# Attention with channels on the partitions, fp32 products and dues from formulas, ahead of a routed MoE and an MLP

## The chip, the cores and the metric

One core of one Trainium2 chip. The metric is the time of one execution on the device in microseconds (us): the median of three runs of the kernel before is 1163.12 us (1162.36 to 1168.79). PE is TensorE (PEld its weight loads), DVE is VectorE, ACT ScalarE, POOL GpSimd, SP SyncE, which issues the DMAs.

## What is computed

Three layers follow one another. The first is a recurrent attention over 768 tokens, for 4 x 8 heads of dimension 40:

```
for t in range(768):
    y[t] = r[t] . state
    Sa = state . a[t]
    state = state * w[t] - Sa (x) b[t] + v[t] (x) k[t]
```

Its output, 3072 rows of 320, goes through a mixture of experts (a skip gate, the argmax of 8 experts, 320 to 1024 to 320 with relu, weighted by the gate and added to the row) and then through an MLP, 320 to 2048 to 320, with g = h / (1 + exp(-1.702 h)).

## The kernel before

**Attention** (class `Attn`, L102) takes 12 chunks of 64 tokens, all 32 heads at a time, and turns the recurrence into matrix products. Within a chunk the decays are normalised at its middle (`g_prep`, scans L244 and L256), a, k and b are scaled by them (`g_a`, `g_kb`), and the products of a with k and b make a triangular system. Tokens lie on the partitions. Operands of TensorE are split into fp16 parts, hi, hi and lo side by side on 120 rows; POOL makes the lo parts (L314, L344, L411, L451, L503, L535, L980), and a, k, b, r, v and the state are turned by transposing DMAs from the SP queue (L319, L351, L541, L708, L719, L984).

**The solve** (`g_gram`, L385 to L402) inverts the 32 x 32 diagonal blocks of all heads of one chunk on DVE. L385 brings the system into Z; Tm starts from a POOL memset (L380) and two ACT copies (L383); then 31 steps follow, each a product tmp <- Tm, Z (L396) and a sum Tm <- Tm, tmp (L399), each waiting for the one ahead of it, all of it in SBUF; L402 turns the inverse back. Its parts go into `te` by DMA.

**The chain** (`g_chain`) makes u of the chunk by products with `te` and `bo` (L593 and others) with ACT copies as parts between them, and then the state after the chunk. `g_pq` and `g_post` make y: the masked products of r with v and u (L738, L741) times km (L763, the one fp32 product of attention), plus the state's share (L766), scaled into xo (L772). `put` (L976 to L998) stores xo as parts for the experts' gather and computes the logits.

**Experts and MLP.** `Moe1` routes the rows, loads and splits the weights, and runs 8 experts (L1263 and others); `Moe2` runs blocks of 512 rows (L1512 to L1515 in, L1552 to L1554 out).

**Order.** Every stage is a generator that yields what its next step takes of an engine (`'P.63*.96'`: 0.63 us of TensorE) or an event or a PSUM slot that it waits for. `weave` (L818) steps them in the order in which they can start by these costs, and among steps that could start nearly together takes the one that is due first. So each engine gets one fixed queue, in order. The dues come from the table `RANK` (L1574), one number for each generator; the formulas in `Attn.DUE` and in the module's `DUE` are there, but not used. `g_warm` issues filler products (L792) where the modelled TensorE pauses. PSUM slots are three of a kind c, three of a kind g (five later), and two of X (gx0, gx1).

## Time and profile before

| what | us |
|---|---|
| median of three runs | 1163.12 |
| span of the profiled execution | 1164.9 |
| PE busy in the span | 929.5 |
| DVE busy | 797.7 |
| ACT busy | 497.2 |
| POOL busy | 473.1 |

The profile shows one execution, whose span is 1164.9 us and whose granted clock is 0.833 on average. Busy times are sums over the span; the stages of this kernel have different limits, so a share of the whole span says little. The columns are read by stage.

### The profile page before, as it was taken

To read this page: it belongs to the slowest core of one execution; us is meant where nothing else is said; L and a number is where in the kernel's file an instruction comes from. 1 tells how busy PE (TensorE), PEld (TensorE's weight loads), DVE (VectorE), ACT (ScalarE), POOL (GpSimd) and SP (SyncE) were. 2 spreads that over 40 slices of the span, in tenths; PEclk is the share of its full clock that TensorE was granted. 3 is DMA by queue.
4 is the path that set the end of the run, shared out by engine and by line. 5 is a ranking of instruction groups with operands and counts; after the bars stand their busy time and mean duration, and the time that the engine had idled before them with its cause. 6 is when DMAs were issued, how large, how long until landed. Compare 5 with 4: busy or idle time off the path is not lost.

```text
span 1164.9 us, 27321 instructions
## 1 busy us (share of the span) xinstructions
PE 929.5 (80%) x11343; PEld 654.4 (56%) x11343; DVE 797.7 (68%) x1655; ACT 497.2 (43%) x987; POOL 473.1 (41%) x405
## 2 busy tenths in 40 slices
PE   5757788598787877968840298995979999999998
PEld 5647667486566675756640176672335555555556
DVE  6599999999999999988658986766972111121110
ACT  2324555445544545436424456442543332333330
POOL 4343345435455544445313635442443332333330
PEclk8776777776777786689855599997989999999999
DMA  6564589799889798865796687434300101010000
GB/s 174 138 152 81 102 169 180 166 160 169 194 154 175 147 186 136 187 111 107 132 258 176 225 192 214 152 130 113 94 26 12 28 22 37 12 29 13 12 12 31
DMA packets 301625, 140.08 MB, mean 120 GB/s; under 512 B 271652, under 2 KB 284712, under 8 KB 299432
## 3 DMA queue, kind: packets, MB, share of 16 engines
q1 hardware_dynamic: 299192, 133.91, 52.8%
q0 software_dynamic: 2304, 4.36, 1.3%
...
## 4 chain that ended last, share of the span: by engine, by line
DVE 37%; PE 37%; DMA 11%; issue 7%; POOL 3%; ACT 3%; SPq 2%; POOLq 0%; DVEq 0%; ACTq 0%
DVE tmp L396 8%; DVE Tm L399 8%; PE c L1552 5%; PE c L1553 4%; PE c L1554 4%; PE g L1512 4%; PE g L1515 3%; PE gx L1512 3%; DMA w2s<-w 3%; PE gx L1515 2%; PE g L763 2%; PE gx L792 2%; DVE pq L741 2%; DMA d_s<-wia 1%; DMA g_x<-xd,g_ig 1%
## 5 line engine op out<-in xcount | busy, mean ns | idle before, releaser
L1535 POOL TENSOR_TENSOR glo<-g,ghi 128x512 f16<-128x512 f32 x96 | 113.8, 1187 | 221.9 <-ACT ghi L1534 221.8
L396 DVE SCALAR_TENSOR_TENSOR tmp<-Tm,Z 128x78 f32<-128x78 f32 (+21 forms) x372 | 148.9, 410 | 8.6 <-ACT Tm L383 3.0
L399 DVE TENSOR_TENSOR Tm<-Tm,tmp 128x78 f32<-128x78 f32 (+21 forms) x372 | 146.7, 405 | 5.1
L792 PE MATMUL gx<-c 128*128 128x192 f16 x840 | 131.6, 300 | 6.4 <-DMA c<-c 3.5
L1531 DVE SCALAR_TENSOR_TENSOR g<-g,sg 128x512 f32<-128x512 f32 x57 | 39.2, 688 | 133.3 <-ACT sg L1529 133.3
L1552 PE MATMUL c<-wo_hi,ghi 128*128 128x320 f16 x384 | 115.9, 302 | 5.9 <-ACT wo_hi L1457 5.9
L1553 PE MATMUL c<-wo_lo,ghi 128*128 128x320 f16 x384 | 115.1, 300 | 0.9 <-DVE wo_lo L1460 0.9
L1554 PE MATMUL c<-wo_hi,glo 128*128 128x320 f16 x384 | 115.2, 300 | 0.0
L792 PEld LDWEIGHTS <-c 128*128 128x128 f16 x840 | 82.0, 116 | 39.5 <-issue 30.1
L1534 ACT CAST ghi<-g 128x512 f16<-128x512 f32 x96 | 59.2, 618 | 76.1 <-DVE g L1531 76.1
L1531 DVE SCALAR_TENSOR_TENSOR g<-gx,sg 128x512 f32<-128x512 f32 x39 | 26.9, 689 | 89.9 <-ACT sg L1529 89.9
L451 POOL TENSOR_TENSOR gkl<-m,gkh 64x512 f16<-64x512 f32 x48 | 58.5, 1218 | 58.7 <-ACT gkh L449 46.4
L1512 PEld LDWEIGHTS <-wi_hi 128*128 128x128 f16 x480 | 45.6, 99 | 60.2 <-DMA xt<-xe 13.3
L763 PE MATMUL g<-km,pq 128*64 128x40 f32 x768 | 58.1, 261 | 26.2 <-DVE pq L741 26.1
L1512 PE MATMUL g<-xt,wi_hi 128*128 128x512 f16 x285 | 71.5, 382 | 1.3 <-DVE g L1531 1.3
L763 PEld LDWEIGHTS g<-km,pq 128*64 128x64 f32 x768 | 54.9, 172 | 29.4 <-DVE pq L741 28.4
L1515 PEld LDWEIGHTS <-wi_lo 128*128 128x128 f16 (+1 forms) x288 | 27.8, 97 | 64.1 <-issue 41.6
L1529 ACT ACTIVATE sg<-g 128x512 f32<-128x512 f32 x57 | 33.7, 595 | 64.2 <-PE g L1515 64.2
L1198 POOL TENSOR_TENSOR w2l<-w2s,w2h 128x1280 f16<-128x1280 f32 x16 | 42.9, 2687 | 44.2 <-ACT w2h L1196 44.0
L1512 PE MATMUL gx<-xt,wi_hi 128*128 128x512 f16 x195 | 49.6, 386 | 12.9 <-DMA xt<-xe 12.9
L1552 PEld LDWEIGHTS <-ghi 128*128 128x128 f16 x384 | 37.5, 98 | 28.6 <-issue 16.1
L1515 PE MATMUL g<-xt,wi_lo 128*128 128x512 f16 x171 | 52.1, 382 | 0.0
...
## 6 DMA issues: line engine op xcount, KB each, us to landing
...
```

The source lines that it names most:

```text
L396: nc.vector.scalar_tensor_tensor(out=tv, in0=Tm[:, r0:, st:st + 1].to_broadcast([128, n, st]), scalar=-2.0 ** -18, in1=Z3[:, st:st + 1, 0: ...
L399: nc.vector.tensor_tensor(out=Tm[:, r0:, 0:st], in0=Tm[:, r0:, 0:st], in1=tv, op=ALU.add)
L763: mm(d, lhsT=self.pq[:, q], rhs=km[:, 40 * p:40 * p + 40], start=h == 0, stop=False, **kw)
L792: self.nc.tensor.matmul(self.X[:, 320:], lhsT=self.C['c_i'][:, 0], rhs=self.C['c_rep'].rearrange('p a b -> p (a b)')[:, :192], start=first ...
L1512: nc.tensor.matmul(h, lhsT=self.whi[:, k % 3, fs], rhs=xt[:, k], start=k == 0, stop=False)
L1515: nc.tensor.matmul(h, lhsT=self.wlo[:p, k, fs], rhs=xt[:p, k], start=False, stop=k == 2)
L1531: nc.vector.scalar_tensor_tensor(out=g, in0=h, scalar=2.0 ** -6, in1=sg2, op0=ALU.mult, op1=ALU.mult)
L1534: nc.scalar.copy(out=ghi[:, f], in_=g)
L1535: nc.gpsimd.tensor_tensor(out=glo[:, f], in0=g, in1=ghi[:, f], op=ALU.subtract)
L1552: nc.tensor.matmul(o, lhsT=ghi[:, f, s], rhs=self.ohi[:, f], start=f == 0, stop=False)
L1553: nc.tensor.matmul(o, lhsT=ghi[:, f, s], rhs=self.olo[:, f], start=False, stop=False)
L1554: nc.tensor.matmul(o, lhsT=glo[:, f, s], rhs=self.ohi[:, f], start=False, stop=f == 15)
```

## The change

Attention is written anew; the code of the experts and the MLP stays, apart from the order in which it is queued.

- Channels, not tokens, lie on the partitions for a, k, b, w and r: the host lays them out so. Products are fp32, so no hi and lo parts are made, and there are no transposing DMAs in attention. What must be turned (the decays F, km, v and u, the state, xo for the logits) goes through TensorE with an identity (L247, L286, L556, L534, L834) and an ACT copy.
- POOL scales a and kb (L261, L275, 1024 elements a partition each) and still makes the lo part of xo in `put`.
- `g_gram` takes a pair of chunks. Z of both (L322) lies side by side, Tm lies in a PSUM bank pair of its own, filled by two matmuls from a constant (L328), and each of the 31 steps is one product (L336) and one subtraction (L339) for both chunks. One Z and one Tm are there, so a pair's Z waits for the solve of the pair ahead, and its Tm for the Tc (L345) of the pair ahead.
- The chain is 5 blocks of 16 products of 64 x 64 with 40 columns for each half of the heads: two into X (L441, L448), then `times` (L462) with tz, bz and tz, one ACT copy between each. `tz` has one buffer, filled from Tc by DMA (L354). Consecutive products of a block go to the two column halves of TensorE by turns (`both`: h outside, par inside).
- The state of both halves is one product with the identity and 16 products per parity (L506, L510), scaled by DVE (L514). y is L575, L577, L598, L603 and L609.
- PSUM slots are four of kind g, six later; c0 and c1 are opened after attention.
- `RANK` goes; `weave(A, z)` takes the dues of the formulas, with `T` = 33 and new numbers in `Attn.DUE`.

Counts in the program: PE instructions with their loads 20888 before, 7866 after; DVE 1666 and 1104; solve operations 744 and 372; fillers 840 and 552.

```diff
-    SLOTS = dict(c=3, g=3, s=1, m=1, v=1, x=1)
...
+    SLOTS = dict(g=4, c=0)
...
+        W = self.tile([128, 2, 1024], F32, 'W', 2)
+        wf, wb = W[:, 0], W[:, 1]
+        nc.vector.tensor_tensor_scan(out=wf, data0=wt[:, 0], data1=C1, initial=0.0, op0=ALU.mult, op1=ALU.add)
...
+        nc.vector.tensor_tensor_scan(out=wb[:, rv], data0=wt[:, 1, rv], data1=C2[:, rv], initial=0.0, op0=ALU.mult, op1=ALU.add)
...
+        self.nc.gpsimd.tensor_tensor(out=t, in0=t, in1=self.ch[c]['W'][:, 0], op=ALU.mult)
...
+        for q in range(2):
+            yield 'G2.4'
+            t = kbT[:, 4 * q:4 * q + 4].rearrange('p a b (e t) -> p (a b) e t', e=2)
+            w = W[:, 4 * q:4 * q + 4].rearrange('p a b t -> p (a b) t').unsqueeze(2).to_broadcast([128, 8, 2, 64])
+            nc.gpsimd.tensor_tensor(out=t, in0=t, in1=w, op=ALU.mult)
...
+                for h in range(4):
+                    nc.tensor.transpose(out=ps[:, 128 * h:128 * h + 128], in_=kbT[:, 4 * q + h, par], identity=self.C['c_id'])
...
+    def g_gram(self, c0):
+        nc, mm = self.nc, self.nc.tensor.matmul
+        pair = range(c0, c0 + 2)
+        for i, c in enumerate(pair):
...
+                yield 'P.9*1.9'
+                Ad = self.pst(sg)
+                for h in range(8):
                     for par in range(2):
+                        for half in range(2):
+                            q = 64 - 64 * par + 32 * half
+                            mm(Ad[q:q + 32, 32 * h:32 * h + 32], lhsT=kbT[r, h, par, q:q + 32],
+                               rhs=at[r, h, par, 32 * half:32 * half + 32], start=True, stop=True)
+                yield 'A.26'
+                nc.scalar.copy(out=Za[:, hb], in_=Ad[:, :256])
                 self.give(sg)
...
+            if not i:
+                yield ('elim', c0 - 2)
+                Z = self.tile([128, 2, 1024], F32, 'Z')
+            yield 'D1.2'
+            nc.vector.transpose(out=Z[:, i], in_=Za.rearrange('p b (g t) -> p t (b g)', t=32).unsqueeze(2).to_broadcast([128, 32, 2, 16]))
+        Z4 = Z.rearrange('p q (s j) -> p q s j', j=32)
+        yield ('tT', c0 - 2)
+        yield 'P.43*1.0'
+        Tm = self.pt.tile([128, 2, 16, 32], F32, name='tm')
         for i in range(2):
+            mm(Tm[:, i].rearrange('p a b -> p (a b)'), lhsT=self.C['c_i'], rhs=self.C['c_tm'], start=True, stop=True)
+        tmp = self.tile([128, 272], F32, 'tmp')
         for st in range(31, 0, -1):
             r0 = st // 2
             n = 16 - r0
+            tv = tmp[:, :2 * n * st].rearrange('p (q a b) -> p q a b', q=2, b=st)
+            d = f'D{.06 + 2 * n * st / 960}'
             yield d
+            nc.vector.tensor_tensor(out=tv, in0=Tm[:, :, r0:, st:st + 1].to_broadcast([128, 2, n, st]),
+                                    in1=Z4[:, :, st:st + 1, 0:st].to_broadcast([128, 2, n, st]), op=ALU.mult)
             yield d
+            nc.vector.tensor_tensor(out=Tm[:, :, r0:, 0:st], in0=Tm[:, :, r0:, 0:st], in1=tv, op=ALU.subtract)
+        self.mark('elim', c0)
+        yield ('te', c0 - 3)
+        Tc = self.tile([128, 2, 512], F32, 'Tc', 2)
+        for i in range(2):
+            yield 'D1.0'
+            nc.vector.transpose(out=Tc[:, i].rearrange('p (g t d) -> p t d g', t=16, d=2), in_=Tm[:, i].rearrange('p a b -> p (a b)'))
+        self.mark('tT', c0)
         yield ('zero', 0)
+        tz = self.tz.rearrange('p (a u) t -> p a u t', a=2)
+        for i, c in enumerate(pair):
+            yield ('U', c - 1)
+            yield 'Q2.4>E1.2'
+            for q in range(4):
+                sl = slice(32 * q, 32 * q + 32)
+                nc.sync.dma_start(out=tz[sl, 1 - q // 2, :, q % 2 * 32:q % 2 * 32 + 32], in_=Tc[sl, i].rearrange('p (u t) -> p u t', t=32))
+            self.mark('te', c)
...
+        for h in range(8):
+            for par in range(2):
+                R = slice(64 * par, 64 * par + 64)
+                nc.tensor.matmul(ps[R, 64 * h:64 * h + 64], lhsT=kbT[r, h, par, R], rhs=at[r, h, par], start=True, stop=True)
         yield 'D.6'
+        m = self.tile([128, 8, 64], F32, f'm{hb}', 2)
...
+        yield 'P.95*1.3'
         X = self.X = self.pst(f'gx{hb}')
+        for h, par, p, d, o in both:
+            mm(X[o, d], lhsT=m[:, h], rhs=vu[:, p], start=h == 0, stop=False, **kw)
+        self.mark(f'Xm{hb}', c)
+        yield ('S', c - 1)
         ST = self.state[c]
+        r = slice(64 * hb, 64 * hb + 64)
+        yield 'P.95*1.3'
+        for h, par, p, d, o in both:
+            mm(X[o, d], lhsT=at[r, h, par], rhs=ST[r, 8 * par + h], start=False, stop=True, **kw)
...
+            w = w.rearrange('p (a u) t -> p a u t', a=2)
+            for h, par, p, d, o in both:
+                mm(z[o, d], lhsT=w[:, par, hb * 8 + h], rhs=t[:, h], start=start and h == 0, stop=True, **kw)
+        yield 'A.33'
+        x = part('x', X, -1.0)
+        yield '+g'
         sc = self.got
+        yield 'P.95*1.3'
         U = self.pst(sc)
+        times(U, self.tz, x, True)
+        yield 'A.33'
+        u = part('y', U, 1.0)
+        yield 'P.95*1.3'
+        times(X, self.bz[c % 2], u, True)
         self.mark(f'B{hb}', c)
+        yield 'A.33'
+        x = part('x', X, -1.0)
         self.mark(f'D{hb}', c)
+        yield 'P.95*1.3'
+        times(U, self.tz, x)
         self.once('U', c)
...
+            mm(ps, lhsT=self.C['c_id'], rhs=ST[:, 8 * par:8 * par + 8].rearrange('p a b -> p (a b)'), start=True, stop=False, **kw)
+            for h in range(8):
+                for hb in range(2):
+                    p = hb * 16 + par * 8 + h
+                    mm(ps[64 * hb:64 * hb + 40, 40 * h:40 * h + 40], lhsT=km[:, p], rhs=vu[:, p], start=False, stop=True, **kw)
...
+        yield 'P.9*1.0'
         ps = self.pst(sg)
+        for j in range(4):
+            i = hb * 8 + par * 4 + j
+            nc.tensor.matmul(ps[:, 128 * j:128 * j + 128].rearrange('p (e t) -> p e t', e=2), lhsT=vt[:, i], rhs=rT[:, :, i], start=True, stop=True)
...
+        yield 'P.95*1.3'
         Y = self.pst(sg)
+        for h in range(8):
+            for par in range(2):
                 d = Y[64 * par:64 * par + 64, 40 * h:40 * h + 40]
+                e = 64 * (h % 2)
+                mm(d, lhsT=self.pq[0][:, 4 * par + h // 2, e:e + 64], rhs=km[:, hb, par, h], start=h == 0, stop=False, **kw)
+        S = self.S
+        yield 'P.95*1.3'
+        for h in range(8):
+            for par in range(2):
+                mm(Y[64 * par:64 * par + 64, 40 * h:40 * h + 40], lhsT=rT[:, h % 2, hb * 8 + par * 4 + h // 2],
+                   rhs=S[:, par * 4 + h // 2, 64 * hb:64 * hb + 40], start=False, stop=True, **kw)
...
+    T = 33.0
+    DUE = dict(zero=-63, load=-75, prep=-66, f=-40, a=-62, kb=-60, gram=-56, ag=-20, ab=-8, v=-20, r=-12, chain=-24, state=-10, sn=4, vt=4, pq=8, post=14, put=22)
...
-RANK = [
-    -404.17427774566124, -491.09060918509874, 1000000000.0, -501.3257727435962, 975.1942770611722, 988.2493608546714, 644.544040243994,
...
-    881.3447098714629, 682.3957237723041, 316.5416932928976, 1095.6692978068609, 1665.069538024102, -225.02167154120986, 383.8421061879434,
-    1343.707675234579, 926.7659247826618, 880.8505466156354, 1708.9576193963935, 887.0972506490499, 582.1332617647189, 2281.6272860544195,
...
                 A.left.close()
                 N.open_out(octx)
+                more = actx.enter_context(tc.tile_pool(name='b_ps', bufs=1, space=PS))
+                A.ps = Banks(A.ps, c0=more, c1=more)
                 M.open_x(xctx, tc, A.ps)
-                for t in ('gx0', 'gx1'):
+                for t in ('gx0', 'gx1', 'c0', 'c1'):
...
-            weave(A, [(d, g) for d, (n, g) in zip(RANK, z)])
+            weave(A, z)
```

Where the solve stands on DVE, before (L385 and L396/L399 of one chunk between those of another; the number at the end of a name is the tile's):

```order
L385 STREAM_TRANSPOSE Z_4148<-g0_4059 128x1024
L772 SCALAR_TENSOR_TENSOR xo_4183<-g2_3946,F_661 128x320
L396 SCALAR_TENSOR_TENSOR tmp_4154<-Tm_4149,Z_4148 128x31
L399 TENSOR_TENSOR Tm_3430<-Tm_3430,tmp_3435 128x14x5
L399 TENSOR_TENSOR Tm_4149<-Tm_4149,tmp_4154 128x31
L396 SCALAR_TENSOR_TENSOR tmp_3435<-Tm_3430,Z_3429 128x56
L396 SCALAR_TENSOR_TENSOR tmp_4154<-Tm_4149,Z_4148 128x30
L399 TENSOR_TENSOR Tm_3430<-Tm_3430,tmp_3435 128x14x4
L399 TENSOR_TENSOR Tm_4149<-Tm_4149,tmp_4154 128x30
L396 SCALAR_TENSOR_TENSOR tmp_3435<-Tm_3430,Z_3429 128x45
L396 SCALAR_TENSOR_TENSOR tmp_4154<-Tm_4149,Z_4148 128x58
```

and after (L322 is Z, L514 the state, L577 and L374 masked products):

```order
L230 TENSOR_TENSOR scl_115<-tots_114 128x8x2
L322 STREAM_TRANSPOSE Z_2724<-Za_3017 128x1024
L514 TENSOR_TENSOR ST_3067<-g0_3171,scl_115 128x320
L336 TENSOR_TENSOR tmp_3200<-tm_3197,Z_2724 128x62
L339 TENSOR_TENSOR tm_3197<-tm_3197,tmp_3200 128x2x31
L336 TENSOR_TENSOR tmp_3200<-tm_3197,Z_2724 128x60
L339 TENSOR_TENSOR tm_3197<-tm_3197,tmp_3200 128x2x30
L336 TENSOR_TENSOR tmp_3200<-tm_3197,Z_2724 128x116
L339 TENSOR_TENSOR tm_3197<-tm_3197,tmp_3200 128x2x2x29
L336 TENSOR_TENSOR tmp_3200<-tm_3197,Z_2724 128x112
L577 TENSOR_TENSOR pq_113<-g1_3225,c_32_86 128x512
L339 TENSOR_TENSOR tm_3197<-tm_3197,tmp_3200 128x2x2x28
```

Before, two chunks' solves of single operations alternate; after, one solve of a pair runs with doubled operations, and other work stands between its steps.

On PE, the end of chunk 3 before the solve of chunks 4 and 5 (L312 the system's products, L506 and L510 the state, L328 the fill of Tm, L448 the state's products into X of chunk 4):

```order
L312 MATMUL g2_3134<-at2_98,kbT1_100 32x32 x32
L506 MATMUL g0_3171<-ST_2568,c_32_86 128x320
L510 MATMUL g0_3171<-vu_2182,km_2059 40x40 x16
L556 MATMUL g1_3191<-c_32_86,vu_2182 80x128 x4
L328 LDWEIGHTS c_16_88
L328 MATMUL tm_3197<-c_16_88 128x512
L328 LDWEIGHTS c_16_88
L328 MATMUL tm_3197<-c_16_88 128x512
L448 MATMUL gx0_3035<-ST_3067,at1_97 64x40 x16
L575 MATMUL g1_3225<-rT1_102,vt_2952 128x128 x4
L286 MATMUL g2_3233<-c_32_86,kbT1_100 128x128 x4
```

The fill of Tm stands behind the state after chunk 3, and the X products of chunk 4 stand right behind it. Before, there is no such fill, and y's products stand so behind those of the chain (L593; L763 with all eight of a parity together, 16 in all, then L766):

```order
L593 LDWEIGHTS te_101
L593 MATMUL c2_4802<-xh0_4757,te_101 128x40
L763 MATMUL g1_4822<-km_1043,pq_108 64x40 x16
L766 LDWEIGHTS rT_4615
L766 MATMUL g1_4822<-S0_3855,rT_4615 64x40
```

The sixteen fp32 products of y go to one column half eight at a time before; after, they alternate.

## Rows read from the trace of the kernel before

**Rows 1.** Stretches: length, then busy us of PE, PEld, DVE, ACT, POOL, PEclk, DMA.
```profile
96.00:562.00 466.00, 371.65 (x7266) 307.28 (x7265) 439.73 (x1046) 234.43 (x548) 221.94 (x200) 0.76 0.81 154
664.00:806.00 142.00, 122.05 (x894) 88.17 (x892) 109.07 (x182) 68.76 (x93) 63.07 (x40) 0.94 0.58 169
```

**Rows 2.** Attention's last DVE step per chunk, and the stores of its rows: counts, first and last start.
```profile
L402 DVE STREAM_TRANSPOSE tmp<-Tm x12: 1034/1049/1091, 96.2 to 562.2; 128x512 f32<-128x512 f32 x12
L772 DVE SCALAR_TENSOR_TENSOR xo<-g,F x24: 427/480/493, 149.7 to 617.3; 128x320 f32<-128x320 f32 x24
L385 DVE STREAM_TRANSPOSE Z<-g x12: 1227/1242/1250, 44.5 to 518.5; 128x1024 f32<-128x1024 f32 x12
```

**Rows 3.** VectorE by line, 96 to 562 us: busy us, mean ns of one.
```profile
L399 DVE TENSOR_TENSOR Tm<-Tm,tmp 128x96 f32<-128x96 f32 (+20 forms) x334 | 133.3, 409 | 4.5
L396 DVE SCALAR_TENSOR_TENSOR tmp<-Tm,Z 128x91 f32<-128x91 f32 (+20 forms) x332 | 131.6, 405 | 8.2 <-ACT Tm L383 3.0 <-DVE Tm L399 0.3 <-DVE tmp L396 0.2
...
L256 DVE TENSOR_TENSOR_SCAN wt<-wt,c_d 128x640 f32<-128x640 f32 x8 | 12.8, 1599 | 0.0
```

**Rows 4.** VectorE from 303.15 us in order of time: start, us, operation.
```profile
303.15 1.18 DVE L396 SCALAR_TENSOR_TENSOR tmp<-Tm,Z 128x81 f32<-128x81 f32 x1
304.37 1.48 DVE L399 TENSOR_TENSOR Tm<-Tm,tmp 128x81 f32<-128x81 f32 x1
...
308.59 0.26 DVE L396 SCALAR_TENSOR_TENSOR tmp<-Tm,Z 128x100 f32<-128x100 f32 x1
308.89 0.26 DVE L399 TENSOR_TENSOR Tm<-Tm,tmp 128x100 f32<-128x100 f32 x1
```

**Rows 5.** GpSimd in the same stretch.
```profile
302.95 1.29 POOL L411 TENSOR_TENSOR Tm<-tmp,Tm 128x512 f16<-128x512 f32 x1 [2.97 <-ACT Tm L409]
304.20 1.54 POOL L340 TENSOR_TENSOR km<-km,FK 128x640 f32<-128x640 f32 x1
```

**Rows 6.** VectorE, two lines with a PSUM source, then one without: ns min/median/max.
```profile
L741 DVE TENSOR_TENSOR pq<-g,c x48: 647/680/692, 143.1 to 606.9; 128x512 f32<-128x512 f32 x48
L1048 DVE TENSOR_TENSOR r_e<-g,c_et x5: 156/191/216, 323.8 to 636.3; 128x64 f32<-128x64 f32 x2, 128x16 f32<-128x16 f32 x2, 128x32 f32<-128x32 f32 x1
L1051 DVE TENSOR_TENSOR r_e<-r_e,r_oh x5: 161/209/2575, 324.1 to 636.7; 128x64 f32<-128x64 f32 x2, 128x16 f32<-128x16 f32 x2, 128x32 f32<-128x32 f32 x1
```

**Rows 7.** TensorE in 280.5 to 282.8 us: fp32 products of y (L763), then L766 between them.
```profile
280.70 1.68 PE L763 MATMUL g<-km,pq 128*64 128x40 f32 x29
...
282.20 0.23 PE L763 MATMUL g<-km,pq 128*64 128x40 f32 x1
282.20 0.22 PE L766 MATMUL g<-S,rT 120*64 120x40 f16 x2
282.26 0.23 PE L763 MATMUL g<-km,pq 128*64 128x40 f32 x1
```

**Rows 8.** The same products at 288.44 us, and the granted clock of both stretches.
```profile
288.44 2.92 PE L763 MATMUL g<-km,pq 128*64 128x40 f32 x29
280.70:282.30 1.60, 1.60 (x39) 1.60 (x37) 1.60 (x4) 1.57 (x4) 0.00 (x0) 1.00 1.14 216
288.40:291.20 2.80, 2.80 (x34) 2.76 (x35) 2.73 (x5) 0.94 (x2) 1.70 (x1) 0.50 1.11 126
```

**Rows 9.** Transposes by TensorE, what starts next, and fillers, in order of time.
```profile
297.30 0.55 PE L269 MATMUL g<-c,wt 128*128 128x128 f32 x3
297.69 0.27 PE L992 MATMUL g<-wgh,xt 128*128 128x9 f16 x5
298.05 1.00 PE L792 MATMUL gx<-c 128*128 128x192 f16 x10
```

**Rows 10.** GpSimd and ScalarE by line, 96 to 562 us.
```profile
L340 POOL TENSOR_TENSOR km<-km,FK 128x640 f32<-128x640 f32 x18 | 28.1, 1563 | 0.2 <-DMA km<-raw 0.2
...
L380 POOL MEMSET Tm<- 128x512 f32 x10 | 5.3, 525 | 1.9 <-DMA te<-Tm 1.6
...
L585 ACT ACTIVATE xl<-gx 128x320 f16<-128x320 f32 x44 | 18.8, 433 | 19.8 <-PE gx L589 17.8 <-PE gx L792 1.5
```

More of the change, by code (lines that the diff above doesn't have):

```diff
@@ L214, in load @@
-    def load(self, n, c):
-        a, w = self.args, dict(wt=1280, am=640, km=1280)[n]
-        src = dict(wt=lambda: a['wt'][c].rearrange('q p a b -> p q (a b)'), am=lambda: a['raw'][c, :, :640],
-                   km=lambda: a['raw'][c, :, 640:])[n]()
-        t = self.tile([128, w], F32, n, self.KM if n == 'km' else 1)
-        t = t.rearrange('p (q x) -> p q x', q=2) if n == 'wt' else t
-        for q in range(2) if n == 'wt' and not c else (slice(None), ):
-            self.nc.sync.dma_start(out=t[:, q], in_=src[:, q])
-        self.ch.setdefault(c, {})[n] = t
@@ new lines, in g_v @@
+        yield ('Sx', c - 2)
+        yield 'Q.6>E3.2'
+        vu = self.tile([128, 32, 40], F32, 'vu', 2)
+        self.nc.sync.dma_start(out=vu.rearrange('p a x -> p (a x)'), in_=self.args['rv'][c])
+        self.ch[c]['vu'] = vu
+        self.mark('v', c)
+    def g_r(self, c):
+        yield ('Y', c - 2)
+        for e in range(2):
+            yield 'Q.6>E.8'
+            self.nc.sync.dma_start(out=self.rT[c % 2][40 * e:40 * e + 40, e].rearrange('p a b -> p (a b)'), in_=self.args['rT'][c, e])
@@ new lines, in g_sn @@
+    def g_sn(self, c):
+        nc = self.nc
+        yield ('S', c)
+        yield ('Y0', c)
+        yield ('Y1', c)
+        S = self.S = self.tile([80, 8, 128], F32, 'S')
+        ST = self.state[c + 1].rearrange('p a b -> p (a b)')
+        for par in range(2):
+            yield '+g'
+            sg = self.got
+            yield 'P.44*.5'
+            ps = self.pst(sg)[:80]
+            for j in range(4):
+                o = 320 * par + 80 * j
+                nc.tensor.transpose(out=ps[:, 128 * j:128 * j + 128], in_=ST[:, o:o + 80], identity=self.C['c_id'])
+            yield 'A.51'
+            nc.scalar.copy(out=S[:, 4 * par:4 * par + 4].rearrange('p a b -> p (a b)'), in_=ps)
+            self.give(sg)
+        self.mark('vs', c)
+        self.mark('Sn', c)
```

852 lines of the change are left out of this document (255 added, 597 removed).

## The prediction

> **What bounds the kernel now.** I cut the span where the solve of a chunk ends on VectorE. Its last step, L402, runs first at 96.2 us and for the twelfth time at 562.2 us [rows 2]: 466 us for 11 chunks, 42.4 us a chunk. In that stretch DVE is busy 439.73 of 466 us, 94%, while PE is busy 371.65 us at a mean granted clock of 0.76, ACT 234 and POOL 222 us [rows 1]. So DVE sets the pace of attention. By line [rows 3], the solve is most of it: L399 and L396 together 264.9 us, 666 operations of 0.41 us. Their price is not their size. In order of time, operations of 81 columns take 1.18 and 1.48 us, and a little later one of 100 columns takes 0.26 us [rows 4]; beside the slow ones POOL runs products of 1.29 and 1.54 us, of nearly the same start and length [rows 5]. The reader is to see there that a solve step with its operands in SBUF stands still while POOL works. The free price fits 0.155 us + columns/960 (0.26 at 100 columns). After the last store of attention's rows, at 617.3 us [rows 2], 548 us follow in code that stays.
>
> All sums are made against the profiled span of 1164.9 us, which stands 1.8 us above the median of 1163.12.
>
> **The change on VectorE.** A pair has 62 operations, each at 0.155 plus a gap of 0.03 us (0.26 us long, the next 0.30 later [rows 4]): 11.5 us. The two operations of the 31 steps pass 11424 columns (of n x st, doubled for the pair), by 960 a us 11.9 us. 23.4 us a pair, 11.7 a chunk, against 24.1 now (264.9 over 11). This needs Tm in PSUM to end the standstill. For it speaks L741, with a PSUM source: 48 times between 0.647 and 0.692 us [rows 6], no stretched one, although POOL was busy half of the time [rows 1]. What else DVE does per chunk: two scans of 1024 columns, by 1.48 us free for 640 (1.6 in the mean [rows 3]) 4.7; Z 1.24 and Tc 1.05; six masks of 0.68, 4.1; state and y 4 x 0.48, 1.9 [rows 2]; small ones 0.6. The parts go (vus, bol, kbs, sm, sh). Sum 25 us a chunk, with both ends 22 (solve covered as above, masks unqueued) and 37 (solve as long as today). DVE no longer bounds.
>
> Does PSUM make a short operation dearer? L1048 reads PSUM and takes 156 to 216 ns, L1051 reads SBUF alone in the same sizes and takes 161 ns at least, 209 in the middle [rows 6]: no difference. [...] I take the rows, at no extra cost.
>
> **POOL, ACT, DMA.** POOL keeps 512 + 1024 + 2048 elements of products, at 1.563 us for 640 [rows 10] 8.7 us, and xo's lo part, 2.1: 11 us a chunk against 20 now. ACT makes some 36 copies of 256 to 512 columns, by 0.433 us for 320 [rows 10] 15 us. SP issues 17 DMAs a chunk (two each for wt, at, kbT and rT, one for vu, four for tz, four stores), and the eight transposing ones are gone. None of the three comes near PE; they count nothing, and if a load were late, PE would wait for it.
>
> **TensorE** becomes the bound. Per chunk, at full clock:
> - 16 blocks of 16 fp32 products with 40 columns (10 in the chain, 2 of a with k, 4 of y). L763 is such a product: 29 records of 52 ns each, 1.68 us, and two records make one product, 104 ns, where eight in a row use one column half [rows 7]. Further on two L766 products for the other half lie between two L763 records, and these start 60 ns apart: what runs in the other half costs 8 ns. With halves by turns a record then costs about 30 ns, a product 59, a block 0.95 us. 16 x 0.95 = 15.2 us. Ends: 0.83 us (two halves in the time of one) and 1.66 us (no overlap).
> - the state: 32 products at 59 ns and two of 320 columns at eight times that, 2.9 us.
> - r with v: 16 products of 128 columns. No row; between 0.14 us (a transpose of that size, 0.13 apart [rows 9]) and 0.28, twice that; I take 0.22, nearer to the upper end as L763 also pays twice: 3.5 us.
> - 96 small products of 32 columns: between 30 and 60 ns, I take 45: 4.3 us. (They have 32 columns where L763 has 40, so the upper end is a pair of its records with the halves by turns, the lower a single one.)
> - 54 transposes at 0.13 us [rows 9], 7.0; logits and the fill of Tm 1.4.
>
> Together 34.3 us, 412 us for 12 chunks. Some 32 us of it stand ahead of the first product with tz, so 380 are left, and about 146 fillers among them at 0.08 us (ten start and end within 1.00 us [rows 9]), 12: 392 us.
>
> [...]
>
> What the clock adds: where PE is kept busy 86% (122.05 of 142 us) the granted clock is 0.94 [rows 1]; with the pauses at chain steps I take 8% on top, 423 us. Cold, the same L763 group takes 2.92 instead of 1.68 us, at a clock of 0.50 against 1.00 [rows 8].
>
> **The head.** Now the first Z starts at 44.5 us [rows 2]. After, POOL clears about 15000 elements a partition, at 0.525 us for 512 [rows 10] 15 us, then two chunks must be scaled before the pair is complete, on shorter paths (no parts, no transposing DMA). I set Z of the pair to about 39 us; solve 23.4 with 10 us of other DVE work between its steps, Tc 2, DMA 5: the first tz product at 79 us. Ends 70 and 95.
>
> **The end.** The last chunk's chain has nothing beside it; 15 us from PE's last bulk to the last xo. 79 + 423 + 15 = 517 us against 617.3: 100 us less. For the 548 us behind it I count nothing: same code, and the order by formulas may cost up to 25 us or gain 10. Span 1065, median **1063 us**. By the bounds above, its own range is 1035 to 1090.
>
> **The rivals.**
> 1. *The solve paces the pairs* (0.20). One Z and one Tm: pair (4, 5) gets its Tm behind the state of chunk 3, and its first tz product stands some 32 us of PE work and 68 fillers (5 us) further on, 40 us at the clock assumed. The solve with other work between, Tc and the DMA needs about the same 40. For it: the queues are in order, and a mask of y between two steps waits for PE. Against it: the sum above just fits. If each pair comes 8 to 15 us late, five pairs add 40 to 75 us: 1103 to 1138. Behind the fill of Tm on PE stand the X products of chunk 4, so a late Tc of the pair ahead stops them too.
> 2. *Column halves do not run side by side for fp32* (0.11). A product then costs 104 ns, 11.5 us more a chunk, 45.8; (12 x 45.8 - 32 + 12) x 1.08 = 572, the last xo at 666 us, 48 us later than now: **1211 us**, slower. It decides from about 89 ns a product (42 us a chunk). For it: the L763 records in one half are as far apart as rows show, and no row has fp32 in both halves at once. Against it: L766 between L763 at 8 ns. A clock that stays at the 0.76 of today's attention does the same to a smaller degree: 392/0.76 = 516, last xo at 610, 1156.
> 3. *The formulas' order hurts the experts and the MLP* (0.10): weights later, blocks further apart, 25 us: 1088.
> 4. *Cheaper yet* (0.09): blocks at 0.83 us, nothing at 8% but 2%, 32.4 us a chunk: (389 - 20) x 1.02 + 85 (head 79, end 6) = 461, last xo 56 us earlier than forecast: 1007.
> That the change doesn't do what it says would mean that the solve's operations stay long from PSUM too, 24 us a chunk: DVE at 37, still under 42, and PE waits for each pair; it is the upper half of rival 1.
>
> **How the numbers follow.** The forecast has 0.50. A measurement of this kernel tells 0.5%, 5.8 us, from no change. Faster by more: forecast, rivals 3 and 4, nearly all of rival 1, 0.87. Within: 0.03, from a rival 1 beyond its span and the clock of 0.76. Slower: 0.10, the rest of rival 2. The range 1015 to 1138 leaves out rivals 2 and 4.
>
> **What would show it.** Right: L336 and L339 never stretched, short of 0.5 us each, their sum near 11 us a chunk; PE busy over 90% of attention at a clock above 0.9; a chain block of 16 products within 0.9 to 1.1 us; last xo between 490 and 545 us; behind it 540 to 575 us. Wrong: PE waiting for the DMA of tz for over 5 us at every second chunk (rival 1); blocks near 1.66 us at clock 1.00 (rival 2); a gap between the last xo and the first expert that exceeds today's 46 us (rival 3). If L336 stretches beside POOL, the step on PSUM fails.

## The result, and the profile after

The changed kernel takes 1134.45 us (median of four runs, 1123.89 to 1152.95), the kernel before 1165.38 in the same rounds: a ratio of 0.970, 95% interval 0.965 to 0.976. The forecast was 1063. The direction is right, and less than a third of the 100 us came. Here and below a median is of all runs of a kernel, and a ratio of its fast runs alone (a run over 1.5% above the fastest of its kernel counts as slow).

The profiled execution spans 1136.1 us, against 1065 forecast. Cut at the first tz product and at the last xo, which is how the sum was made (columns as in rows 1: length, busy us of PE, PEld, DVE, ACT, POOL, granted clock, DMA share, GB/s):

```profile
0.00:115.30 115.30, 80.46 (x1450) 72.67 (x1450) 79.48 (x111) 15.70 (x38) 58.51 (x34) 0.78 0.36 95
115.30:591.30 476.00, 452.49 (x9478) 405.43 (x9477) 273.42 (x582) 163.52 (x403) 122.78 (x98) 0.86 0.29 83
591.30:1136.10 544.80, 472.70 (x2828) 271.93 (x2828) 241.61 (x378) 211.57 (x340) 194.17 (x145) 0.93 0.26 78
```

| part | forecast | measured | difference |
|---|---|---|---|
| head, to the first tz product | 79 | 115.3 | +36.3 |
| from there to the last xo (392 of work, 31 of clock, 15 of end) | 438 | 476.0 | +38.0 |
| behind it, no change counted | 547.6 | 544.8 | -2.8 |

TensorE has taken VectorE's place as the bound: it is busy 452 of 476 us, DVE 273 (before, DVE 94% and PE 80% of its stretch [rows 1]). And the granted clock is 0.86 there. 0.86 x 476 is 409 us at full clock (waits included, and good to some 2 us, as the clock has two digits), against 392 + 15 = 407 forecast. So the sum was sized right; what is missing is 36 us of head and 36 us of clock (67 lost, 31 counted).

TensorE in order of time, where the clock was 1.00 (start, us, operation; two records make one product):

```profile
317.39 2.05 PE L575 MATMUL g<-rT,vt 80*128 80x128 f32 x16
319.37 2.06 PE L462 MATMUL g<-x,tz 128*64 128x40 f32 x64
321.26 2.04 PE L462 MATMUL gx<-y,bz 128*64 128x40 f32 x64
323.13 1.11 PE L598 MATMUL g<-km,pq 128*64 128x40 f32 x32
324.06 2.28 PE L462 MATMUL g<-x,tz 128*64 128x40 f32 x64
```

Two blocks of the chain, 64 records, start 1.89 and 1.87 us apart from what follows, so 0.94 us a block, and L598's takes 0.93; 0.95 was forecast, from rows in which only fp16 products ran between [rows 7]. Eight products of r with v take 1.98 us, 0.25 each, where 0.22 was taken.

The solve, and Z (count, ns min/median/max, first and last start):

```profile
L336 DVE TENSOR_TENSOR tmp<-tm,Z x186: 181/366/500, 69.9 to 502.0; 128x252 f32<-128x252 f32 x18, 128x60 f32<-128x60 f32 x12, 128x112 f32<-128x112 f32 x12, 128x156 f32<-128x156 f32 x12
...
L339 DVE TENSOR_TENSOR tm<-tm,tmp x186: 189/372/450, 70.2 to 502.2; 128x252 f32<-128x252 f32 x18, 128x60 f32<-128x60 f32 x12, 128x112 f32<-128x112 f32 x12, 128x156 f32<-128x156 f32 x12
...
L322 DVE STREAM_TRANSPOSE Z<-Za x12: 1821/1935/2017, 44.2 to 471.3; 128x1024 f32<-128x1024 f32 x12
```

The steps of the solve before, over the whole span:

```profile
L396 DVE SCALAR_TENSOR_TENSOR tmp<-Tm,Z x372: 155/264/2933, 48.1 to 561.4; 128x126 f32<-128x126 f32 x18, 128x56 f32<-128x56 f32 x13, 128x78 f32<-128x78 f32 x13, 128x96 f32<-128x96 f32 x13
L399 DVE TENSOR_TENSOR Tm<-Tm,tmp x372: 138/268/2630, 48.7 to 561.6; 128x126 f32<-128x126 f32 x18, 128x96 f32<-128x96 f32 x14, 128x56 f32<-128x56 f32 x13, 128x78 f32<-128x78 f32 x13
```

No step of the solve takes over 0.50 us, where single ones took 1.18 and 1.48 [rows 4] and the longest 2.93. Of the 372 steps 91 run beside a GpSimd operation, and the longest of these takes 0.44 us; before, 116 of 744 took over 0.50 us, each of them beside one, and none of the others over 0.41. Of VectorE's larger steps Z was mis-sized most: 1.94 us from SBUF where it took 1.24 from PSUM [rows 2].

**The clock.** TensorE's queue around 126 us, then VectorE's, then the granted clock:

```profile
125.63 0.69 PE L399 MATMUL g<-at,kbT 64*32 64x32 f32 x32
128.96 0.81 PE L506 MATMUL g<-ST,c 128*128 128x320 f32 x2 [2.63 <-DVE ST L514]
```

```profile
128.10 0.42 DVE L339 TENSOR_TENSOR tm<-tm,tmp 128x240 f32<-128x240 f32 x1
128.42 0.48 DVE L514 TENSOR_TENSOR ST<-g,scl 128x320 f32<-128x320 f32 x1
```

```profile
120.00:128.00 8.00, 6.33 (x196) 5.49 (x192) 7.45 (x20) 3.42 (x8) 0.00 (x0) 1.00 0.59 118
130.00:140.00 10.00, 10.00 (x168) 8.44 (x161) 6.49 (x16) 3.34 (x7) 0.00 (x0) 0.52 0.15 33
140.00:170.00 30.00, 30.00 (x419) 28.36 (x419) 12.77 (x30) 4.41 (x11) 7.90 (x5) 0.50 0.22 66
180.00:240.00 60.00, 60.00 (x1380) 54.09 (x1380) 17.41 (x23) 24.59 (x64) 12.44 (x10) 1.00 0.27 80
```

TensorE waits 2.63 us for the state's step L514, which stands in VectorE's queue behind steps of the next pair's solve. The clock is 1.00 ahead of the pause and 0.50 from 130.5 us on, for 48 us, in which TensorE is busy without a gap. It comes back at 178 us, behind transposes (L556, L534, L834) and a group of L399 that run from 173.6 us. The same happens at 410 us (a pause of 1.38 us for L514, then 0.50 for 41 us) and, for 17 us, at 277 us in the last us of a pause of 5.4 us for the routing. These three low stretches cost 24, 20 and 9 us, 53 of the 67. But a pause of 2.2 us at 453 us is followed by 11 us at 1.00, up to the next, and this one, of 2.3 us at 466 us, by 7 us at 0.50. The four runs of the one program show the same sum: clock times span is 1007, 1008, 1004 and 1010 us, while the times differ by 29 us. What differs between them is the clock.

### The profile page after: what moved, and what is told of

Read it like the earlier page. It is cut to its first block, busy times and chain, and to the rows that moved or that the text cites. A ratio compares the mean times of both kernels' runs of the same rounds, so it can differ in the third digit from the quotient of the medians.

```text
span 1136.1 us, 30957 instructions
## 1 busy us (share of the span) xinstructions
PE 1005.6 (89%) x13755; PEld 750.0 (66%) x13755; DVE 594.5 (52%) x1070; ACT 390.8 (34%) x780; POOL 375.5 (33%) x277
## 4 chain that ended last, share of the span: by engine, by line
PE 71%; DVE 13%; DMA 7%; issue 3%; POOL 3%; ACT 1%; SPq 1%; DVEq 0%; POOLq 0%; ACTq 0%
PE g L1360 5%; PE c L1400 4%; PE g L575 4%; PE c L1401 4%; PE c L1402 4%; PE g L462 4%; PE g L1363 3%; PE gx L1360 3%; PE gx L448 2%; PE g L371 2%; PE g L598 2%; PE g L603 2%; PE g L286 2%; PE gx L441 2%; PE g L556 2%
## 5 line engine op out<-in xcount | busy, mean ns | idle before, releaser
L275 POOL TENSOR_TENSOR kbT<-kbT,W 128x1024 f32<-128x1024 f32 x24 | 66.2, 2771 | 48.0 <-DMA kbT<-kbT 29.2
L339 DVE TENSOR_TENSOR tm<-tm,tmp 128x252 f32<-128x252 f32 (+22 forms) x186 | 65.9, 354 | 4.8
L336 DVE TENSOR_TENSOR tmp<-tm,Z 128x252 f32<-128x252 f32 (+22 forms) x186 | 64.7, 348 | 4.7 <-PE tm L328 0.2
L628 PE MATMUL gx<-c 128*128 128x192 f16 x552 | 60.3, 271 | 3.5 <-DMA c<-c 3.5
L1363 PE MATMUL g<-xt,wi_lo 128*128 128x512 f16 (+1 forms) x192 | 59.2, 385 | 0.0
L1111 PE MATMUL g<-g_xt,w1h 128*128 128x240 f16 x220 | 31.4, 275 | 30.9 <-DMA g_xt<-g_x 30.9
L462 PE MATMUL g<-x,tz 128*64 128x40 f32 x1536 | 56.8, 239 | 2.1 <-issue 2.0
L575 PE MATMUL g<-rT,vt 80*128 80x128 f32 x384 | 58.2, 310 | 0.0
L462 PEld LDWEIGHTS g<-x,tz 128*64 128x64 f32 x1536 | 53.2, 149 | 6.0 <-issue 4.1
L575 PEld LDWEIGHTS g<-rT,vt 80*128 80x128 f32 x384 | 52.5, 217 | 1.5
```

The lines of the kernel that those rows point to most:

```text
L275: nc.gpsimd.tensor_tensor(out=t, in0=t, in1=w, op=ALU.mult)
L339: nc.vector.tensor_tensor(out=Tm[:, :, r0:, 0:st], in0=Tm[:, :, r0:, 0:st], in1=tv, op=ALU.subtract)
L462: mm(z[o, d], lhsT=w[:, par, hb * 8 + h], rhs=t[:, h], start=start and h == 0, stop=True, **kw)
L575: nc.tensor.matmul(ps[:, 128 * j:128 * j + 128].rearrange('p (e t) -> p e t', e=2), lhsT=vt[:, i], rhs=rT[:, :, i], start=True, stop=True)
L628: self.nc.tensor.matmul(self.X[:, 320:], lhsT=self.C['c_i'], rhs=self.C['c_tm'][:, :192], start=first, stop=True, skip_group_check=True)
L1363: nc.tensor.matmul(h, lhsT=self.wlo[:p, k, fs], rhs=xt[:p, k], start=False, stop=k == 2)
```

## The experiments

Two theories were to be told apart for the stretch: pauses of TensorE bring the clock down, and it stays down; or the products themselves, or chance, do it. For the head: the pair waits for chunk 1 and for loads; or VectorE and GpSimd set its pace in any case. Product below is clock times length of the stretch from the first tz product to the last xo, in the run that was traced; for the changed kernel it is 409 us.

**A pause put in, and the same pause filled.** First edit:

```diff
             yield 'D.38'
-            nc.vector.tensor_tensor(out=STn[:, 8 * par:8 * par + 8], in0=ps.rearrange('p (h d) -> p h d', d=40),
+            for i in range(11 if c == 5 and par else 1):
+              nc.vector.tensor_tensor(out=STn[:, 8 * par:8 * par + 8], in0=ps.rearrange('p (h d) -> p h d', d=40),
...
```

> After, with one pause put in where there was none: VectorE's step for the second half of the state behind chunk 5 (L514) is done eleven times over, same operands and result, some 5 us more before TensorE gets the state for chunk 6. In the trace of the changed kernel this place (about 340 us) lies in 100 us of granted clock 1.00. Theory (a pause of TensorE of some 2 to 4 us is enough, and the clock then stays at 0.50 for 10 to 45 us while TensorE is busy): behind the pause clock 0.50 for at least 10 us, that stretch of the profile longer by the pause plus 5 to 22 us. Rival (the low stretches come at their own times, whatever TensorE did): clock 1.00 behind the pause, cost the 3 to 5 us of the pause alone.

Second edit, on top of it (queued behind the transposes that stand there, ahead of L448):

```diff
+        if not hb and c == 6:
+            for i in range(64):
+                mm(X[:, 320:], lhsT=self.C['c_i'], rhs=self.C['c_tm'][:, :192], start=False, stop=True, **kw)
```

> The same eleven steps, and 64 filler products (fp16, 128 x 192, 0.08 us each at full clock, 5 us) in TensorE's queue behind the wait's other work, ahead of the state's products of chunk 6, so that TensorE works through the time. The order of everything else is that of the run with the pause alone. Theory: clock stays 1.00 behind this place, and the stretch costs the 5 us of fillers and no more. Rival (low clock at its own times, or by VectorE's work): as in the run with the pause alone.

With the pause, TensorE's queue and the clock of the stretches around:

```profile
361.70 0.30 PE L448 MATMUL gx<-ST,at 64*64 64x40 f32 x2
366.61 1.93 PE L448 MATMUL gx<-ST,at 64*64 64x40 f32 x30 [4.61 <-DVE ST L515]
```

```profile
350.00:360.00 10.00, 10.00 (x185) 8.40 (x183) 5.16 (x13) 4.90 (x13) 5.58 (x4) 1.00 0.39 110
366.60:380.00 13.40, 13.39 (x216) 12.54 (x218) 1.38 (x2) 2.17 (x6) 2.03 (x1) 0.50 0.09 26
380.00:400.00 20.00, 20.00 (x296) 19.13 (x295) 1.88 (x3) 4.24 (x11) 1.25 (x3) 0.50 0.15 32
407.00:430.00 23.00, 23.00 (x488) 20.87 (x486) 6.00 (x8) 9.09 (x23) 1.24 (x4) 0.97 0.32 93
```

With the pause filled:

```profile
350.72 5.44 PE L446 MATMUL gx<-c 128*128 128x192 f16 x64
...
356.53 1.13 PE L451 MATMUL gx<-ST,at 64*64 64x40 f32 x32
```

```profile
340.00:350.00 10.00, 10.00 (x197) 8.45 (x198) 4.76 (x11) 4.89 (x13) 5.58 (x4) 1.00 0.44 109
350.00:380.00 30.00, 30.00 (x730) 28.40 (x724) 9.63 (x18) 9.29 (x23) 4.00 (x5) 1.00 0.23 62
380.00:400.00 20.00, 20.00 (x430) 18.00 (x428) 5.78 (x8) 7.67 (x21) 1.17 (x3) 1.00 0.31 100
```

The same place, the same eleven steps on VectorE: with a pause of 4.61 us the clock is 0.50 for 40 us, with TensorE at work it stays at 1.00. Both spend some 5 us at the place itself, waiting or with fillers; 40 us at half the clock are 20 more, and the medians are 1157.07 and 1136.08 us (products 409 and 417, with the fillers). In this pair of traces it is the pause that sets off the low clock, and not VectorE's work or the place. It is one trace of each, and the pause need not cost as much every time: the four runs with it took 1130.38 to 1170.18 us, and the fastest lost 117 us to the clock over its whole span (span times what is missing to 1.00), no more than the runs of the changed kernel (112 to 147); the other three lost 139 to 160. Nor does each pause bring the clock down: of the six of 1 to 2 us that these two traces have between 115 and 560 us with the clock at 1.00 in the 5 us ahead, five are followed by a mean clock of 0.58 to 0.91 in the next 3 us, and one, of 1.09 us at 419 us with the pause filled, by 1.00.

A pause of a microsecond isn't needed either. In the trace of a run further below (chunks one by one, 10 fillers, r later) the longest wait of TensorE in the 10 us ahead of a low stretch of 44 us is this:

```profile
190.06 0.78 PE L454 MATMUL gx<-ST,at 64*64 64x40 f32 x19 [0.58 <-issue]
...
192.30:236.70 44.40, 44.40 (x620) 40.30 (x617) 19.12 (x38) 8.84 (x23) 4.59 (x6) 0.50 0.20 61
```

So a pause can set off the low clock; that nothing else does isn't shown, and the second theory (the products themselves, or chance) stays open beside the first.

**Order of the halves.** Edit: `for par in range(2) for h in range(8)` in the chain's blocks, in y and in a with k, instead of h outside.

> After, with the 16 products of a block in another order: all eight of one column half, then all eight of the other (160 chain, 64 of y and 32 of a with k per chunk). Theory (fp32 products of the two halves overlap; the trace has a block of 32 records at 0.93 to 1.08 us at full clock): blocks at about 1.66 us, 16 x 0.65 = 10 us more per chunk, time about 1134 + 125 = 1260, at least 1220. Rival (the order doesn't matter, a record costs 29 to 34 ns in either): within 10 us of 1134.

1287.73 us (1240.88 to 1296.14); blocks at full clock:

```profile
386.34 3.13 PE L462 MATMUL g<-x,tz 128*64 128x40 f32 x61
...
389.45 2.93 PE L462 MATMUL gx<-y,bz 128*64 128x40 f32 x58
```

58 records take 2.93 us, the last one 0.23 of it: 47 ns a record, 1.5 us a block, against 0.94. The product is 517 us, 108 more over 192 blocks, 0.56 each. The halves do overlap in fp32, and rival 2 of the forecast falls by its own mechanism.

**Fillers ahead of the state's products.**

```diff
+        if not hb and c:
+            yield ('Sx', c - 1)
+            yield 'P2.3*2.3'
+            for i in range(28):
+                mm(X[:, 320:], lhsT=self.C['c_i'], rhs=self.C['c_tm'][:, :192], start=False, stop=True, **kw)
         yield ('S', c - 1)
```

> After, plus 28 filler products (fp16, 128 x 192, some 2.3 us at full clock) in the TensorE queue of each chunk, ahead of the state's products into X (L448), where the trace of the changed kernel shows TensorE waiting 1.4 to 2.6 us for the state and the granted clock at 0.50 for some 45 us behind two of these waits (129 to 174 us, 408 to 452 us). Theory (these pauses bring the clock down, and the low clock takes some 45 of the 74 us that are missing): mean clock of 115 to 592 us goes from 0.86 to 0.92 or more, time 1134 to about 1095 to 1120 in spite of 11 x 2.3 = 25 us of fillers, part of which fills the pauses. Rival (the clock falls by what the fp32 products are, not by the pauses): clock as before, time 10 to 30 us longer.

1142.06 us (ratio to before 0.980, 0.972 to 0.987). The clock of the stretch rose to 0.92, as the theory said, but the product to 444: an estimated 25 us of fillers (308 of 0.08 us) and some waiting were paid for 28 us of clock (39 lost, not 67). The time expected by the theory was missed; the time is nearer to the rival's.

**VectorE waits instead.** In the model, the state's product counts as done 2.5 us earlier, so L514 is queued earlier.

```diff
-            yield 'P1.6*1.9'
+            yield hint('P1.6*1.9', -2.5)
```

> After, with one thing changed in the model that makes the queues: a product of the state (L510) is taken as done 2.5 us earlier, so that VectorE's step for the state (L514) stands earlier in VectorE's queue and VectorE, which is busy 55% of attention, waits for TensorE there, and not TensorE for VectorE. No filler is added. Theory (the pauses at L448, some 1.4 to 2.6 us, bring the clock down): waits of TensorE for L514 nearly gone, mean clock of 115 to 592 us 0.90 or more against 0.86, time 1134 to about 1100 to 1120. Rival (other pauses, or the products themselves, bring the clock down as often): clock 0.85 to 0.88, time within 10 us of 1134.

```profile
116.60:573.00 456.40, 431.42 (x9456) 385.23 (x9455) 273.32 (x580) 163.57 (x402) 120.74 (x99) 0.91 0.30 85
```

1125.99 us (0.964, 0.960 to 0.969): clock 0.91, product 415. The waits for L514 are shorter, not gone (up to 1.8 us), and one pause for a mask, 2.9 us at 232 us, still was followed by 44 us at 0.50. Above the time expected, with the clock as expected; the interval touches the changed kernel's (0.965 to 0.976), so in time the gain isn't clear.

**Costs as measured.** The durations of the trace in the model by which the queues are made.

> After, with the costs by which the queues are made set to the durations of its trace: Z 1.9 instead of 1.2 us, masks 0.66 for 0.6, the products of a and kb on GpSimd 4.2 and 3.3 for 2.4, a block on TensorE 1.0 for 0.95, four transposes 0.56 for 0.44, copies of ScalarE 0.42 for 0.33. Theory (TensorE pauses where the order assumed another engine to be done): fewer pauses over 1 us than the 6 of the changed kernel, clock of attention 0.90 or more, time 1095 to 1125. Rival (pauses move to other places): within 10 us of 1134.

```profile
112.30:553.90 441.60, 420.34 (x9494) 378.33 (x9493) 273.63 (x582) 163.61 (x404) 127.90 (x99) 0.93 0.33 90
```

1111.32 us (0.950, 0.947 to 0.954): first tz product at 112.3, clock 0.93, product 411. It has nine pauses over 1 us where the changed kernel, counted alike, has eight, so not fewer; but the low stretches that begin ahead of 533 us are short, 7 to 14 us. The time is within the range expected, the way there is another.

**No fillers at all.**

```diff
-            if owed > 0.0:
+            if owed > 0.0 and False:
```

> After without its 552 filler products (L628). Theory (the clock follows TensorE's pauses, and fillers shorten them): clock of attention lower, time 1134 plus 10 to 40. Rival (fillers stand in the way: 146 of them behind the first tz product cost 12 us): 1134 less 5 to 15.

1139.59 us (0.978, 0.973 to 0.983): clock 0.83, product 399. In the traced run clock and product both fall; over the whole span its four runs have clocks of 0.882 to 0.903, the changed kernel's 0.872 to 0.900, so a lower clock isn't shown. The intervals of this and of the changed kernel touch, so in time it is open which is better, and both expectations missed.

**Tm in SBUF.**

```diff
+        yield 'A.9'
+        Tm = self.tile([128, 2, 16, 32], F32, 'tms')
+        nc.scalar.copy(out=Tm, in_=Tp)
```

> After, with Tm copied by ScalarE from PSUM to SBUF once a pair, and the 62 operations of the solve on it there. It undoes the place of Tm alone. Theory (a step with both sources in SBUF stands still while GpSimd works, one with a source in PSUM does not): the median of L336 as now, its longest over 1.2 us against 0.50 now, sum of the solve 20 to 60% above 131 us; time 1134 plus 5 to 30, as TensorE and not VectorE sets the pace. [...]

```profile
L339 DVE TENSOR_TENSOR tmp<-tms,Z x186: 190/366/3172, 68.8 to 517.2; 128x252 f32<-128x252 f32 x18, 128x60 f32<-128x60 f32 x12, 128x112 f32<-128x112 f32 x12, 128x156 f32<-128x156 f32 x12
...
L342 DVE TENSOR_TENSOR tms<-tms,tmp x186: 202/374/3120, 71.0 to 517.4; 128x252 f32<-128x252 f32 x18, 128x60 f32<-128x60 f32 x12, 128x112 f32<-128x112 f32 x12, 128x156 f32<-128x156 f32 x12
```

The median of L336's counterpart is 366 ns in both, its longest 3.17 us from SBUF against 0.50 from PSUM, and the solve's sum 162 against 131 us, 24% more. 19 of the 372 steps took over 0.55 us, and each of them ran beside a GpSimd operation. So in these traces the standstill beside GpSimd comes with both sources in SBUF, and with one in PSUM it is gone. That PSUM makes a step dearer isn't seen: the medians are equal, and the shortest steps take 181 ns with PSUM and 190 from SBUF alone. Time 1145.93 us (0.980, 0.974 to 0.985).

**The first two chunks one by one.**

```diff
-            if c % 2 == 0:
-                gens += [(d('gram'), self.g_gram(c))]
+            if c < 2:
+                gens += [(d('gram'), self.g_gram(c, 1, c - 1, c - 2))]
+            elif c % 2 == 0:
...
```

> After, with the first two chunks solved one by one, the others in pairs as before. Theory (the head is long because the first pair waits for chunk 1, whose system is there at 66 us against 44 us for chunk 0): first tz product at 70 to 90 us instead of 115, last store of attention's rows 20 to 35 us earlier, time about 1100 to 1115. Rival (what the first chunks' other work on VectorE, GpSimd and the DMAs takes sets the pace of the first 200 us): first tz product earlier, but the chunks behind it no earlier, time within 10 us of 1134.

```profile
0.00:97.20 97.20, 64.56 (x1194) 57.94 (x1194) 64.77 (x112) 14.76 (x36) 53.25 (x33) 0.79 0.38 105
97.20:548.70 451.50, 427.80 (x9606) 383.74 (x9605) 288.27 (x633) 163.44 (x404) 122.84 (x99) 0.92 0.31 87
548.70:1101.50 552.80, 474.13 (x2830) 273.08 (x2829) 250.32 (x389) 212.16 (x341) 208.47 (x147) 0.93 0.26 78
```

1119.12 us (0.960, 0.954 to 0.965), just above the time expected, in runs of 1103.28 to 1156.79; the trace is of the fastest. The first tz product comes at 97.2, less early than expected: scans and masks of the next chunks stand between the steps of the first solve, which ends at 83.9 us, and TensorE's queue has other work ahead of the product. The last xo is 43 us earlier: 18 from the head, the rest from the clock (0.92, product 415). What follows takes 8 us longer.

**r loaded later.** In the changed kernel SyncE's queue has this (start of the issue):

```profile
3.27 0.36 SPq L195 DMA_DIRECT2D wt<-wt  x1
...
10.86 0.30 SPq L422 DMA_DIRECT2D rT<-rT  x1
...
12.97 0.33 SPq L195 DMA_DIRECT2D wt<-wt  x1
```

```diff
         yield ('Y', c - 2)
+        yield ('W', min(c, 1))
         for e in range(2):
```

> After, with one edit: the loads of r (rT) for the first two chunks are issued only behind the decays of chunk 0 and 1. In the changed kernel's SyncE queue the first of them stands ahead of the second half of wt of chunk 0 and waits there for GpSimd's clearing of rT (9.0 to 12.5 us): the first half of wt is issued at 3.3 us, the second at 13.0, and the first scan starts at 20.7. Theory (9 of the 36 us by which the head was longer than forecast are this wait): first scan at 10 to 13 us, first tz product 5 to 9 us earlier than 115.3, time less by as much as far as the clock's stretches let it be seen (c x span: clock times span lower by 5 to 9). Rival (the loads land no earlier, or GpSimd is late with a and kb anyway): first scan earlier, first tz product within 3 us of 115.3.

```profile
13.86 2.29 DVE L212 TENSOR_TENSOR_SCAN W<-wt,c_d 128x1024 f32<-128x1024 f32 x1 [4.22 <-DMA at<-at]
...
58.79 1.98 DVE L322 STREAM_TRANSPOSE Z<-Za 128x1024 f32<-128x1024 f32 x1 [0.68 <-ACT Za L315]
...
109.04 3.64 PE L463 MATMUL g<-x,tz 128*64 128x40 f32 x64
```

The first scan starts at 13.9 us instead of 20.7, and the first tz product at 109.0 instead of 115.3: 6.3 us of the 36. The time, 1129.80 us (0.970, 0.959 to 0.980), doesn't show it within its spread, nor does clock times span, 1010 to 1013 us against 1004 to 1010. One of the four runs took 3573.68 us at a clock of 1.00; why isn't known. The other three are 1109.49, 1121.52 and 1138.07 us.

**Edits together.** The first: chunks 0 and 1 one by one, L514 queued earlier, the routing's product later.

> After, with three edits together: the first two chunks solved one by one, the state's step of VectorE queued 2.5 us earlier, and the product of the routing (L892), for which TensorE waited 5.4 us with the clock falling behind it, queued 6 us later. Theory (head and pauses add up): 1119 of the run with the first two chunks alone, less 15 to 30: 1085 to 1105, runs closer together, clock of attention 0.92 or more. Rival (the clock falls in any case, at other places): 1110 to 1125, spread of the runs as wide as before.

1137.83 us (1117.51 to 1143.44), clock 0.89 to 0.91 in its runs but for one of 0.88; the head is as short (98.3), but pauses came up elsewhere (at 188 and 287 us), and the part behind the last xo grew to 567 us. Both expectations missed; an edit on one pause moves the others.

The second: chunks 0 and 1 one by one, 10 fillers ahead of the state's products.

> After, with the first two chunks solved one by one, and 10 fillers (0.8 us) ahead of the state's products of each chunk. Theory (the shorter head and the shorter low stretches add up, at a cost of 9 us for fillers): time 1095 to 1112 with the runs closer together than the 1103 to 1157 of the first edit alone. Rival (fillers cost what they bring): 1115 to 1130.

```profile
0.00:99.60 99.60, 71.12 (x1194) 63.64 (x1194) 62.05 (x114) 14.77 (x36) 51.58 (x33) 0.73 0.36 103
99.60:551.10 451.50, 433.17 (x9724) 388.49 (x9723) 302.31 (x638) 164.75 (x404) 120.98 (x100) 0.94 0.32 87
551.10:1104.70 553.60, 474.65 (x2828) 272.70 (x2828) 244.03 (x381) 211.65 (x341) 199.49 (x145) 0.93 0.27 78
```

**1104.12 us** (1091.74 to 1107.97; 0.944, 0.938 to 0.949), better than both kernels: clock 0.94, product 424 with 9 us of fillers. The runs lie together, as expected.

With r loaded later on top:

> The three edits that helped or should help together: the first two chunks solved one by one, 10 fillers ahead of the state's products, r loaded behind the first decays. Theory (the head's two parts add): 1104 of the run with the first two, less 5 to 9: 1095 to 1100. Rival (behind the first pair the head is set by GpSimd and VectorE, not by the loads): within 4 us of 1104.

1103.81 us (0.944, 0.938 to 0.951): no gain over the one before, as the rival had it, though the first tz product comes at 94.4 instead of 99.6.

Costs, fillers and r, in pairs:

> After, with the measured costs, 10 fillers ahead of the state's products and r loaded behind the first decays, all pairs. Theory (pauses and head add up): 1111 of the run with the costs alone, less 5 to 9 for r, less what the fillers bring (nothing to 10): 1095 to 1106, clock of attention 0.93 or more. Rival: fillers cost 9 us where few pauses are left: 1108 to 1118.

1124.58 us (0.965, 0.959 to 0.971), more than with the costs alone; both expectations missed. Its trace, too, has 41 us at a clock of 0.50 (from 463.8 us) with no wait over 0.45 us in the 17 us ahead of them.

**Before, by its formulas.** `weave(A, z)` in the kernel before.

> Before, with nothing changed but the dues: the formulas that stand in it instead of the table. It tells what the loss of the table is worth in a kernel that is otherwise the same. Theory (VectorE sets the pace before, so the order counts for the pauses only): 1165 plus 10 to 50 us. Rival (the table is worth nothing): within 6 us of 1165. If it is far over 50 us, the changed kernel paid for the formulas too, and a table for it could gain as much.

1175.79 us (1.008, 1.005 to 1.011): the table was worth some 9 us there, about the least that the theory expected. It isn't known what one would be worth to the changed kernel.

## Why the prediction was right and wrong

**Right:** the bound. The solve left the path: 131 us for 12 chunks, 10.9 a chunk (11.7 forecast), no step stretched, and the run with Tm in SBUF shows that this is due to PSUM (there the longest took 3.17 us, and the steps 162). TensorE's work at full clock, 407 forecast with the end, 409 found, with the block at 0.94 to 1.07 us. That the sum fits so well is partly luck: its 96 small products took 2.9 us a chunk (two groups each of L312, 0.76 us, and L399, 0.69) where 4.3 were taken, which paid for blocks that took some 1.0 us instead of 0.95 and for r with v at 4.0 instead of 3.5. The part behind attention, 544.8 against 547.6. Rival 1, the solve pacing the pairs, didn't come: behind the first tz product none of the changed kernel's pauses over 1 us is put down to Tc or to the DMA of tz. The one that is, 12.1 us for Tc at 101 us, belongs to the head. Rival 2 is refuted by the order of the halves.

**Wrong, the clock term:** "with the pauses at chain steps I take 8% on top, 423 us". 67 us were lost instead of 31. The 0.94 was read from a stretch of another code and taken as what a busy TensorE is granted; but the clock here is lost in a few stretches at 0.50 (48, 17, 41 and 7 us, and the first 17 us of one from 574 us on), while TensorE is busy 95% of the time (452 of 476 us). Of the five that begin behind the first tz product, four begin in a single pause of 1.38 to 5.4 us or up to 2.3 us behind it, the fifth, at 574 us, among waits of 0.3 to 0.9 us. Rival 2's last sentence had the case of a clock of 0.76, as something that lasts, not as something that comes behind a wait of 2.6 us. The step that failed is this term: it priced the pauses by little more than their own length, where three of them, of 1.4 to 5.4 us, were followed by losses of 9 to 24 us. What else can start such a stretch, and why some pauses start none, stays open. The pauses come where TensorE's queue assumed another engine to be done: the state behind VectorE's solve steps and Z, the routing behind a stretched copy (L878, 2.10 us at 276 us, 0.17 at 455).

**Wrong, the head:** "I set Z of the pair to about 39 us". The second Z of the pair starts at 66.2 and the solve ends at 109.4, not at 72 (VectorE; then GpSimd):

```profile
20.66 2.29 DVE L212 TENSOR_TENSOR_SCAN W<-wt,c_d 128x1024 f32<-128x1024 f32 x1 [11.02 <-DMA wt<-wt]
...
44.22 1.94 DVE L322 STREAM_TRANSPOSE Z<-Za 128x1024 f32<-128x1024 f32 x1
...
66.21 1.97 DVE L322 STREAM_TRANSPOSE Z<-Za 128x1024 f32<-128x1024 f32 x1 [4.41 <-ACT Za L315]
...
69.92 0.21 DVE L336 TENSOR_TENSOR tmp<-tm,Z 128x62 f32<-128x62 f32 x1
...
109.39 1.04 DVE L345 STREAM_TRANSPOSE Tc<-tm 128x512 f32<-128x512 f32 x1
```

```profile
24.80 4.43 POOL L261 TENSOR_TENSOR at<-at,W 128x1024 f32<-128x1024 f32 x1
33.87 6.62 POOL L275 TENSOR_TENSOR kbT<-kbT,W 128x1024 f32<-128x1024 f32 x2 [4.64 <-DMA kbT<-kbT]
...
42.23 4.23 POOL L261 TENSOR_TENSOR at<-at,W 128x1024 f32<-128x1024 f32 x1
51.28 6.65 POOL L275 TENSOR_TENSOR kbT<-kbT,W 128x1024 f32<-128x1024 f32 x2 [4.83 <-DMA kbT<-kbT]
```

Chunk 0's Z comes at 44.2, near its place before [rows 2], but the pair needs chunk 1's, 22 us later: its scan waits 8.8 us for a load into the one buffer of wt, and a and one of the two products of kb take GpSimd 4.2 to 4.4 us, each with a scan beside it for over 2 us, not 2.5 (in the whole trace those without take 2.3 to 2.4). That is 27 of the 36 us. The solve took 39.5 us instead of 33.4, as two chunks' scans stand in it, 6 more; Z itself and the masks ahead of the first step make the rest. Of the 27, some 7 are the load of r (the second Z starts at 58.8 without it), whose place in SyncE's queue the forecast counted but didn't follow.
